# Attention and a mixture of experts on one core: the issue order of all engines worked out by the kernel's own list scheduler

## The chip, the cores and the metric

The kernel runs on one core of a Trainium2 chip. A core has TensorE (PE in the profile; its weight loads are PEld), VectorE (DVE), ScalarE (ACT), GpSimd (POOL) and SyncE (SP), which issues all of this kernel's DMA transfers. Each engine takes its instructions in one fixed order. The metric is the device time of one execution in microseconds; less is better.

## The reference

Two parts are chained. Attention with a local window and block summaries (batch 4, 8 heads, 768 positions, head size 64) gives x, 3072 tokens of 512; a dense mixture of four experts works on x.

```python
k_sum = k.reshape(B, H, nb, block, D).max(axis=3)      # block = 32
v_sum = v.reshape(B, H, nb, block, D).mean(axis=3)
scores_l = scale * q @ k.T      # kept where abs(i - j) < 16, else -1e9
scores_s = scale * q @ k_sum.T + np.log(block)
a = softmax(concat[scores_l, scores_s])
x = a @ concat[v, v_sum]
...
p = domain_probs / (domain_probs.sum(-1, keepdims=True) + 1e-09)
for e in range(4):
    h = np.maximum(x @ w1[e], 0.0)        # 512 -> 1024
    out += p[:, e:e + 1] * (h @ w2[e])    # 1024 -> 512
```

All is float32. The kernel splits operands into a high and a low part and adds three products.

## The kernel before

**Attention** is cut into 64 pieces `n`: batch `n // 16`, 96 queries, four heads. A piece goes through these steps (names as in the code and the profile): `load_piece` (transfers `kr` with keys, `qv` with queries and values), `stage_a` (ACT and POOL split them into `ks`, `qs`, `v12`), `scores` (PE products `psc`, the maximum `nb` on DVE, the exponential `ms` on ACT), `probs` (DVE and ACT write the weights `aw`, high and low), `transposed` (a transposing transfer to `awT`, issued by SP), `values` (PE products `px`), `to_x` (ACT and DVE bring `px` out as `xs`; `xh` and `xl` are its parts). Pieces 0 to 7 have a path of their own (`first_tokens`), with an order written as a table of times (`KEYS`, `STEPS`). Before the pieces of a batch `b` come its summaries: `setup_k` and `setup_v` load eight chunks (`kch`, `vch`), reduce them on DVE (`ksr`, `vsr`, `vmax`), and `setup_v` works out a scale with two small PE steps, `pmx`, and transposes `pvs`.

**The experts** work on blocks of 384 tokens. Blocks 0 and 1 take plain products (`plain_units`): `ph` = w1 x, out as `hh`, `hl`; `po` = w2 h, added into `acc`. Raw weights come in as `wr`, and `w` holds the parts. Blocks 2 to 7 go in three pairs (`pair_units`), whose first product is made with seven half-size products instead of eight (`first`, table `SEVEN`): PSUM banks `pha` to `phd`, with an ACT copy from `pha` to `phb` (the start of the second bank), DVE sums `phb + p` into `phc` and `phd`, and operands `w1g` and `x_t` that ACT, POOL and DVE prepare from `wx` and `xr`. There are 48 such blocks (pair, expert, quarter). The last pair does so for the second product too (`second_sevens`, `poa` to `pod`). Weight scales need two small PE steps per expert, `pmw`.

**What sets the order.** The code interleaves both parts: `advance` issues attention steps up to a position that grows with the expert work done, piece by piece, by the tables `ENDS` and `SHIFT`. The tile framework then orders the instructions of each engine with a scheduler of its own, which may reorder whatever is not pinned by `tc.keep_in_program_order`. Pinned are: everything in the first stage (up to the flags set at lines 1284 and 1289), the loads in `load_chunk` (line 201) and `load_raw` (line 818), and the instructions that prepare w2 in `fetch7` (line 970). Evictions of PSUM in the pairs stand under `tc.high_priority(offset=RUSH)`. All instructions run through the wrapper `Engine` (line 67), so nearly all rows of the profile have its line, L75, and go by tile names. The part that decides on pinning:

```python
def issue(*a, **kw):
    ins = getattr(self.engine, name)(*a, **kw)
    if pinned[self.which]:
        tc.keep_in_program_order(ins)
    return ins
```

`to_x` (line 429) takes the two halves of `px` so: ACT scales half 1 into `xs`, DVE scales half 0 and adds.

Of the kernel before, what the change touches and what calls it, by code (L numbers as in the profile page):

```python
# [2 lines left out]

# [5 lines left out]
F32 = mybir.dt.float32  # L9
F32R = mybir.dt.float32r  # L10
BF16 = mybir.dt.bfloat16
F16 = mybir.dt.float16
AF = mybir.ActivationFunctionType
ALU = mybir.AluOpType
AX = mybir.AxisListType

P = 128
B, H, S, D = 4, 8, 768, 64
# [40 lines left out]
    return min(max(QB * i - WIN, 0), S - KW)  # L59


@with_exitstack
def attn_moe(ctx: ExitStack, tc: tile.TileContext, qvL, qv0, v0L, kD, kT, vT, w1L, w2L, dpL, cst, out):
    nc = tc.nc
    pinned = {"load": True, "rest": True}

    class Engine:


        def __init__(self, engine, which):  # L70
            self.engine, self.which = engine, which

        def __getattr__(self, name):
            def issue(*a, **kw):
                ins = getattr(self.engine, name)(*a, **kw)  # L75
# [6 lines left out]
    V, A, PL, PE = (Engine(e, "rest") for e in (nc.vector, nc.scalar, nc.gpsimd, nc.tensor))  # L82
    SP = Engine(nc.sync, "load")

    def pool(name, bufs=1, **kw):
        return ctx.enter_context(tc.tile_pool(name=name, bufs=bufs, **kw))

    const = pool("const")

    def spare_x(n):  # L90
# [3 lines left out]
    sb = pool("sb")  # L94
# [75 lines left out]
    def mixing():  # L170
        SP.dma_start(pw, dpL)
        s = const.tile([P, NT, 1], F32, name="dps")
# [25 lines left out]
    written = {}  # L198
    st = {}

    def load_chunk(b, hp, ch, src):
        tc.keep_in_program_order(
            nc.sync.dma_start(ch, src[b, 2 * hp : 2 * hp + 2].rearrange("h d s -> (h d) s"))
        )
# [81 lines left out]
    def load_piece(n):  # L286
# [142 lines left out]
    def to_x(n):  # L429
        i, g = (n // 2) % NQ, n % 2  # L430
        tb, ib = n // per, i % (TB // QB)
        pxv = st.pop(n)["px"]
        xs = sb.tile([P, 2, QB], F32, name=f"xs{n}", tag="xt", bufs=2)
        by = 1.0 / ASC if tb < 2 else X_TOP / (ASC * V_TOP)
        A.mul(xs, pxv[:, :, 1, :], by)
        V.scalar_tensor_tensor(xs, pxv[:, :, 0, :], by, xs, op0=ALU.mult, op1=ALU.add)
        if tb < 2:
            if tb not in xT:
                xT[tb] = x_block(tb)
            xh, xl = (x[:, :, ib * QB : (ib + 1) * QB] for x in xT[tb][g])  # L440
# [292 lines left out]
        vmean0.append(v0)  # L733


    RUSH = 200
    SLOW = 0.6
    US1, US2 = 0.175, 0.231

# [78 lines left out]
    def load_raw(e, pr):  # L818
        if (e, pr) in raw_w1 or (e, pr, "1") in stored:
            return  # L820
        raw_w1[e, pr] = []
        for j in range(2):
            raw = sb.tile([P, 512], F32, name=f"wx{e}_{2 * pr + j}", tag="x", bufs=NX)
            tc.keep_in_program_order(nc.sync.dma_start(raw, w1L[e, 2 * pr + j]))
            raw_w1[e, pr].append(raw)

    def w1_operands(e, pr):
# [66 lines left out]
    acc, added = {}, {}  # L894
    scaled_pw = {}
    xpair = {}
    kept = {}
# [44 lines left out]
    es_of = dict(PAIRS)  # L942
    orders, todo, ready = {}, [], {}
# [26 lines left out]
    def fetch7():  # L970
        if todo7:
            e, i = todo7.pop(0)
            pinned["rest"] = True
            w2_operands(e, i, *(("chunk", CHUNKS) if i == 3 and e != es_of[SEVENS[0]][0] else ("x", NX)))
            pinned["rest"] = False

    ready2 = {}

# [116 lines left out]
    def second_sevens(pr, tbs, e, hs):  # L1095
        for t in range(TB // P):
            bank = {}

            def new(k):
                room, tag = dict(a=(ps_sc, "sc"), d=(ps_av, "av")).get(k, (ps_mm, "mm"))  # L1100
                bank[k] = room.tile([P, 512], F32, name=f"po{k}{pr}_{e}_{t}", tag=tag)[:, :256]
                return bank[k]

            gts = [tb * (TB // P) + t for tb in tbs]
            if e == es_of[pr][0]:
                for gt in gts:
                    acc[gt] = sb.tile([P, DM], F32, name=f"acc{gt}", tag="acc", bufs=6)

            def add(row, col, k):
                gt = gts[row]  # L1110
                pe = scaled_pw[e][:, gt % (S // P)]
                to = acc[gt][:, col * 256 : (col + 1) * 256]
                if e == es_of[pr][0]:
                    V.tensor_scalar_mul(to, bank[k], pe)
                else:
                    V.scalar_tensor_tensor(to, bank[k], pe, to, op0=ALU.mult, op1=ALU.add)

            for m, (k, h, w) in enumerate(SEVEN):
# [9 lines left out]
                with tc.high_priority(offset=RUSH):  # L1128
                    if m == 0:
                        A.copy(new("b"), o)  # L1130
                    elif m == 1:
                        five = sb.tile([P, 256], F32, name=f"q5{pr}_{e}_{t}", tag="hs", bufs=2)
                        A.copy(five, o)
                    elif m == 2:
                        V.tensor_tensor(new("c"), o, five, op=ALU.add)
                    elif m == 3:
                        add(0, 0, "a")
                    elif m == 4:
                        V.tensor_tensor(bank["d"], o, five, op=ALU.add)
                        add(1, 1, "d")  # L1140
                    elif m == 5:
                        add(0, 1, "c")
                    else:
                        add(1, 0, "b")
                    if e == es_of[pr][-1] and m > 4:
                        gt = gts[m - 5]
                        SP.dma_start(out[gt * P : (gt + 1) * P, :], acc.pop(gt))
# [43 lines left out]
    def first(pr, tbs, e, hT, w2, room):  # L1191
# [6 lines left out]
            op0=ALU.mult, op1=ALU.mult,  # L1198
        )
        order = orders[pr, e]  # L1200
        for n, i in enumerate(order):
# [6 lines left out]
            bank = {}  # L1208
            at = dict(ops=hT)
# [6 lines left out]
            for m, (k, w, x) in enumerate(SEVEN):  # L1216
                first = m < 2
                o = new(k) if first else bank[k]
# [7 lines left out]
                ahead_of = ExitStack()  # L1226
                ahead_of.enter_context(tc.high_priority(offset=RUSH))
# [20 lines left out]
                ahead_of.close()  # L1248
# [6 lines left out]
    steps = []  # L1255
    for n in range(per, NTB * per):
        k = n + SHIFT * (n >= 2 * per)
# [35 lines left out]
    for (tbs, experts), end in zip(plan, ENDS):  # L1295
        pair = tbs if isinstance(tbs, int) else None
        n = 2 if pair else len(tbs)
# [5 lines left out]
        parts, u, done = None, 0.0, 0.0  # L1303
# [82 lines left out]
```

## Time and profile before

| | |
|---|---|
| median of 3 runs | 1166.38 us (1165.22 to 1167.75) |
| the profiled execution | 1163.23 us, span 1161.5 us |
| PE, DVE, ACT, POOL busy | 1102.4, 818.6, 692.7, 550.8 us |
| mean granted TensorE clock | 0.975 |
| transfers | 184.10 MB, mean 159 GB/s |

An engine's idle time before an instruction stands in brackets with what released it. A row of a stretch gives its bounds, its length, the busy time of PE, PEld, DVE, ACT and POOL with the number of instructions, the granted clock, the DMA share and GB/s.

### The profile page before, as it was taken

Reading aid. Unit: us, or ns where it says so; the run is one execution under the profiler, and the core shown is the slowest. Engines: PE = TensorE matmul, PEld = TensorE weight load, DVE = VectorE, ACT = ScalarE, POOL = GpSimd, SP = SyncE. Lnnn points to the kernel's source line nnn. Section 1 sums busy time; section 2 is a strip of 40 time slices with the busy share of each in tenths; the row PEclk is TensorE's granted clock in tenths of the full one; section 3 lists DMA queues with packets and bytes.
Section 4 is the critical chain, followed back from the end, with each engine's and each line's share of the span. In section 5 each row is a group of like instructions: output and inputs, shape, how many; then the busy total and the mean of one; then the engine's idle time right before and its main releaser. Section 6 shows DMA issues by size and latency. Waiting matters only on the chain.

```text
span 1161.5 us, 20511 instructions
## 1 busy us (share of the span) xinstructions
PE 1102.4 (95%) x6994; PEld 758.6 (65%) x6994; DVE 818.6 (70%) x1959; ACT 692.7 (60%) x1882; POOL 550.8 (47%) x650
## 2 busy tenths in 40 slices
PE   9899688999999789999979999999999999999998
PEld 7788587898896455545544555555555458686867
DVE  6888878875787797676786545456643568787784
ACT  5667466674556888776755445455532356666661
POOL 2587555773744998575653321233300134344340
PEclk9999888999999799999989999999999999999999
DMA  6476756663748599575774536465451142323201
GB/s 241 137 213 179 192 145 184 171 176 89 218 133 212 174 332 311 181 243 166 230 285 120 165 100 191 119 199 152 117 166 36 64 139 80 123 95 125 68 15 55
DMA packets 169305, 184.10 MB, mean 159 GB/s; under 512 B 79344, under 2 KB 115184, under 8 KB 169200
## 3 DMA queue, kind: packets, MB, share of 16 engines
q1 hardware_dynamic: 169200, 182.79, 52.1%
q8 instruction: 55, 0.90, 0.3%
q14 instruction: 50, 0.41, 0.1%
HBM read 131.76 MB, written 34.08 MB: 143 GB/s over the span
## 4 chain that ended last, share of the span: by engine, by line
PE 37%; DVE 6%; DMA 4%; ACT 2%; issue 2%; POOL 1%; SPq 0%; POOLq 0%; ACTq 0%; DVEq 0%
PE po L75 14%; PE phb L75 8%; PE pha L75 5%; PE phc L75 3%; PE phd L75 3%; DVE wr L75 2%; PE poa L75 1%; PE pob L75 1%; PE psc L75 1%; DMA wr<-in_w2L 1%; DVE acc L75 1%; DMA kch<-in_kT 1%; PE pod L75 1%; PE px L75 1%; DMA vch<-in_vT 1%
## 5 line engine op out<-in xcount | busy, mean ns | idle before, releaser
L75 PEld LDWEIGHTS <-w1g 128*128 128x128 f16 x2016 | 196.1, 99 | 155.3 <-issue 21.8
L75 PE MATMUL po<-w2s,h 128*128 128x512 f16 x1152 | 271.2, 379 | 1.2 <-DVE acc L75 0.7
L75 PEld LDWEIGHTS <-h 128*128 128x128 f16 x1584 | 152.4, 98 | 125.9 <-issue 1.4
L75 PE MATMUL phb<-x_t,w1g 128*128 128x384 f16 x864 | 166.2, 330 | 7.3 <-DVE phd L75 4.5
L75 PE MATMUL ph<-xh,w 128*128 128x384 f32 x512 | 144.2, 352 | 10.8 <-ACT xh L75 3.8
L75 POOL TENSOR_TENSOR ks<-kr,ks 128x304 fp32r<-128x304 f32 x112 | 99.3, 892 | 111.3 <-ACT ks L75 110.4
L75 PE MATMUL po<-w,hh 128*128 128x512 f32 x384 | 122.0, 396 | 0.0
L75 ACT ACTIVATE ms<-ms,nb 96x152 f32<-96x152 f32 x256 | 104.3, 415 | 25.6 <-DVE nb L75 24.6
L75 PE MATMUL pha<-x,w1g 128*128 128x384 f16 x576 | 114.5, 333 | 4.9 <-DVE nb L75 4.8
L75 POOL TENSOR_TENSOR w<-wr,w 128x512 fp32r<-128x512 f32 x60 | 81.2, 1363 | 54.9 <-ACT w L75 51.8
L75 PEld LDWEIGHTS ph<-xh,w 128*128 128x128 f32 x512 | 97.9, 197 | 13.4 <-ACT xh L75 4.2
L75 POOL TENSOR_TENSOR v<-qv,v 128x256 f16<-128x256 f32 (+1 forms) x56 | 42.3, 756 | 120.4 <-ACT v L75 108.3
L75 DVE CUSTOM_DVE_ANT_0 ms<-psc,c_sb 96x152 f32<-96x152 f32 x256 | 69.2, 305 | 39.5 <-PE psc L75 36.4
L75 PE MATMUL ph<-xl,w 128*128 128x384 f32 x256 | 89.0, 348 | 0.0
L75 PEld LDWEIGHTS po<-w,hh 128*128 128x128 f32 x384 | 70.9, 189 | 14.6
L75 ACT CAST aw<-ms 96x512 f16<-96x512 f32 x112 | 49.5, 488 | 50.6 <-issue 21.7
L75 DVE TENSOR_TENSOR aw<-ms,aw 96x512 f16<-96x512 f32 x112 | 70.4, 661 | 11.5 <-ACT aw L75 11.2
L75 POOL TENSOR_TENSOR w2g<-wr,w2g 128x256 f16<-128x256 f32 (+1 forms) x32 | 29.5, 939 | 99.6 <-ACT w2g L75 99.3
L75 PE MATMUL po<-w,hl 128*128 128x512 f32 x192 | 76.3, 398 | 0.0
L75 PE MATMUL psc<-ks,qs 128*96 128x152 f32 x448 | 64.9, 271 | 6.6 <-POOL qs L75 3.6
L75 ACT CAST w<-wr 128x512 fp32r<-128x512 f32 x84 | 51.0, 616 | 32.4 <-DMA wr<-in_w1L 21.1
L75 ACT CAST ks<-kr 128x304 fp32r<-128x304 f32 x112 | 48.1, 442 | 33.4 <-PE psc L75 29.7
(184 smaller groups left out, 2251.6 us busy)
## 6 DMA issues: line engine op xcount, KB each, us to landing
wr<-in_w2L SPq DMA_DIRECT2D x104, 256.0 KB, 3.2
qv<-in_qvL SPq DMA_DIRECT2D x56, 320.0 KB, 3.7
kr<-in_kD SPq DMA_DIRECT2D x56, 256.0 KB, 3.2
w1g<-wdg SPq DMA_DIRECT2D x28, 512.0 KB, 3.6
wr<-in_w1L SPq DMA_DIRECT2D x44, 256.0 KB, 3.0
w1g<-wdg SPq DMA_DIRECT2D x28, 384.0 KB, 3.6
wx<-in_w1L SPq DMA_DIRECT2D x32, 256.0 KB, 3.8
wd<-w2s SPq DMA_DIRECT2D x16, 512.0 KB, 5.5
```

The costliest lines, as they stand in the source:

```text
L75: ins = getattr(self.engine, name)(*a, **kw)
```

## The change

The wrapper no longer issues. It appends a `Step` to a list `program`, with the engine, the call, the tiles it writes and reads, and two durations from linear formulas (`takes`, how long the engine is held; `lasts`, until the result is there). At the end `order_of` turns the list into an order, and every instruction is issued in it and pinned:

```diff
 def issue(*a, **kw):
-    ins = getattr(self.engine, name)(*a, **kw)
-    if pinned[self.which]:
-        tc.keep_in_program_order(ins)
-    return ins
+    program.append(Step(self.key, lambda: getattr(self.engine, name)(*a, **kw), name, a, kw))
...
+    for n in order_of(program, bufs_of):
+        tc.keep_in_program_order(program[n].issue())
```

`order_of` has three parts. It finds the dependences from the tiles' footprints and the rotation of each tag's buffers (a new tile waits until all users of the one it replaces are done). It works out due times backwards: PE's steps have their place in program order as a nominal time, and any other step is due by the earliest consumer less durations and waits. Then it lists: each engine takes, at the time it comes free, the ready step with the smallest rank.

```diff
+WAIT = dict(PE=53, ACT=33, DVE=33, POOL=76, SP=28)
+SPARE, SPARE_DMA, LANES = 0.1, 300.0, 8
...
+    def POOL(self, op, kw):
+        n = self.moved()
+        t = 250.0 + 2.1 * n if op == "tensor_tensor" else 100.0 + 1.5 * n
+        return t * (1 + SPARE), t * (1 + SPARE) + 10.0
...
+        due[n] = min(nominal.get(n, math.inf), *d) if d else nominal.get(n, math.inf)
+        if due[n] == math.inf:
+            due[n] = place + 30000.0
+    rank = [nominal.get(n, due[n]) for n in range(len(steps))]
...
+        n = heapq.heappop(waiting[k])[1]
+        s = steps[n]
+        order.append(n)
+        free[k] = t + s.takes
+        if k == "SP":
+            wire = end = max(wire, t + s.lasts[0]) + s.lasts[1]
+            lanes = [*lanes[1:], end]
+        else:
+            end = t + s.lasts
```

The durations of DVE, ACT and POOL are raised by a tenth, transfers by a fifth and 300 ns. All transfers pass one `wire` one after another, eight under way at most. The flags of `pinned` and the blocks under `tc.high_priority` are gone; the tables and `advance` stay, and give the program order that PE's ranks are taken from. In `to_x` the halves change places:

```diff
-        A.mul(xs, pxv[:, :, 1, :], by)
-        V.scalar_tensor_tensor(xs, pxv[:, :, 0, :], by, xs, op0=ALU.mult, op1=ALU.add)
+        A.mul(xs, pxv[:, :, 0, :], by)
+        V.scalar_tensor_tensor(xs, pxv[:, :, 1, :], by, xs, op0=ALU.mult, op1=ALU.add)
```

Both kernels hold the same instructions on every engine; the order differs. In rows of the order, ISA is the operation that adds the mask and takes the maximum of the scores, and the last number in a name only counts tiles.

More of the change, by code (lines that the diff above doesn't have):

```diff
@@ L1 @@
+import heapq
 import math
 from contextlib import ExitStack
+from functools import cache
 import concourse.bass as bass
@@ L59, in _win0, with columns, footprint @@
     return min(max(QB * i - WIN, 0), S - KW)
+BYTES = {F32: 4, F32R: 4, F16: 2, BF16: 2}
+WAIT = dict(PE=53, ACT=33, DVE=33, POOL=76, SP=28)
+SPARE, SPARE_DMA, LANES = 0.1, 300.0, 8
+def columns(ap):
+    return math.prod(n for _, n in ap.ap[1:])
+@cache
+def footprint(offset, pairs, wide):
+    (step, parts), *rest = pairs
+    mask = (1 << wide) - 1
+    for s, n in reversed(rest):
+        if s and n > 1:
+            one, mask = mask, 0
+            for k in range(n):
+                mask |= one << (s * wide * k)
+    return offset // step, offset // step + parts, mask << (offset % step * wide)
@@ new lines, in order_of, with loosen, give @@
+def order_of(steps, bufs):
+    used, live = {}, {}
+    for n, s in enumerate(steps):
+        seen = {}
+        for ap, w in [(x, True) for x in s.written] + [(x, False) for x in s.read]:
+            name, tag = ap.tensor.name, getattr(ap.tensor, "tag", None)
+            if tag is None:
+                continue
+            p0, p1, mask = footprint(ap.offset, ap.ap, BYTES[ap.dtype] // 2)
+            kept = []
+            for at in live.get(name, ()):
+                m, a0, a1, was, wrote = at
+                if m != n and (w or wrote) and a0 < p1 and p0 < a1:
+                    chain = s.key == "PE" == steps[m].key
+                    if was & mask or chain:
+                        full = not chain and (wrote or steps[m].key != s.key)
+                        s.behind[m] = max(s.behind.get(m, False), full)
+                        if w and not was & ~mask and a0 >= p0 and a1 <= p1:
+                            continue
+                kept.append(at)
+            live[name] = [*kept, (n, p0, p1, mask, w)]
+            seen[name] = tag
+        for name, tag in seen.items():
+            used.setdefault(tag, {}).setdefault(name, []).append(n)
+        s.tiles = list(seen.items())
+        for m, full in s.behind.items():
+            steps[m].ahead.append((n, full))
+    queue = {tag: sorted(tiles, key=lambda t: tiles[t][0]) for tag, tiles in used.items()}
+    nominal, now = {}, 0.0
+    for n, s in enumerate(steps):
+        if s.key == "PE":
+            nominal[n] = now
+            now += s.takes
+    freed = {}
+    for tag, names in queue.items():
+        for old, new in zip(names, names[bufs[tag] :]):
+            first = used[tag][new][0]
+            for m in used[tag][old]:
+                if m < first:
+                    freed.setdefault(m, []).append(first)
+    due, place = {}, now
+    for n in range(len(steps) - 1, -1, -1):
+        s = steps[n]
+        place = nominal.get(n, place)
+        end = sum(s.lasts) if s.key == "SP" else s.lasts
+        d = [due[m] - (end + WAIT[steps[m].key] if full else s.takes) for m, full in s.ahead]
+        d += [due[m] - end - WAIT[steps[m].key] for m in freed.get(n, ())]
+        due[n] = min(nominal.get(n, math.inf), *d) if d else nominal.get(n, math.inf)
+        if due[n] == math.inf:
+            due[n] = place + 30000.0
+    rank = [nominal.get(n, due[n]) for n in range(len(steps))]
+    left = [len(s.behind) + len(s.tiles) for s in steps]
+    ready = [0.0] * len(steps)
+    uses = {name: len(at) for tiles in used.values() for name, at in tiles.items()}
+    gone, given = {}, {}
+    coming = {k: [] for k in WAIT}
+    waiting = {k: [] for k in WAIT}
+    free = dict.fromkeys(WAIT, 0.0)
+    lanes, wire, order = [0.0] * LANES, 0.0, []
+    def loosen(n, t):
+        ready[n] = max(ready[n], t)
+        left[n] -= 1
+        if not left[n]:
+            heapq.heappush(coming[steps[n].key], (ready[n], n))
+    def give(tag, t):
+        k = given[tag] = given.get(tag, -1) + 1
+        if k < len(queue[tag]):
+            for n in used[tag][queue[tag][k]]:
+                loosen(n, t + WAIT[steps[n].key] if t else 0.0)
+    for n, s in enumerate(steps):
+        if not left[n]:
+            heapq.heappush(coming[s.key], (0.0, n))
+    for tag in queue:
+        for _ in range(bufs[tag]):
+            give(tag, 0.0)
+    while len(order) < len(steps):
+        best = None
+        for k in WAIT:
+            t = max(free[k], lanes[0] + WAIT[k]) if k == "SP" else free[k]
+            while coming[k] and coming[k][0][0] <= t:
+                n = heapq.heappop(coming[k])[1]
+                heapq.heappush(waiting[k], (rank[n], n))
+            if not waiting[k]:
+                if not coming[k]:
+                    continue
+                t = coming[k][0][0]
+            if best is None or t < best[0]:
+                best = t, k
+        t, k = best
+        while coming[k] and coming[k][0][0] <= t:
+            n = heapq.heappop(coming[k])[1]
+            heapq.heappush(waiting[k], (rank[n], n))
+        n = heapq.heappop(waiting[k])[1]
+        s = steps[n]
+        order.append(n)
[3 more added lines that the diff above has]
+            lanes = [*lanes[1:], end]
+        else:
+            end = t + s.lasts
+        for m, full in s.ahead:
+            loosen(m, end + WAIT[steps[m].key] if full else t + 1.0)
+        for name, tag in s.tiles:
+            uses[name] -= 1
+            gone[name] = max(gone.get(name, 0.0), end)
+            if not uses[name]:
+                give(tag, gone[name])
+    return order
@@ L823, in load_raw @@
             raw = sb.tile([P, 512], F32, name=f"wx{e}_{2 * pr + j}", tag="x", bufs=NX)
[L824 removed]
+            SP.dma_start(raw, w1L[e, 2 * pr + j])
             raw_w1[e, pr].append(raw)
@@ L1127, in second_sevens @@
                     PE.matmul(o, hl, wh, start=False, stop=i == FC // 2 - 1, **again)
[L1128 to L1147, printed above, removed]
+                if m == 0:
+                    A.copy(new("b"), o)
+                elif m == 1:
+                    five = sb.tile([P, 256], F32, name=f"q5{pr}_{e}_{t}", tag="hs", bufs=2)
+                    A.copy(five, o)
+                elif m == 2:
+                    V.tensor_tensor(new("c"), o, five, op=ALU.add)
+                elif m == 3:
+                    add(0, 0, "a")
+                elif m == 4:
+                    V.tensor_tensor(bank["d"], o, five, op=ALU.add)
+                    add(1, 1, "d")
+                elif m == 5:
+                    add(0, 1, "c")
+                else:
+                    add(1, 0, "b")
+                if e == es_of[pr][-1] and m > 4:
+                    gt = gts[m - 5]
+                    SP.dma_start(out[gt * P : (gt + 1) * P, :], acc.pop(gt))
                 if (t, m) in ((0, 3), (0, 6), (1, 2), (1, 5)):
```

92 lines of the change are left out of this document (75 added, 17 removed).

## The prediction

> **What bounds the kernel now.** I read the page first, then busy time by stretches, then the gaps on PE one by one.
>
> ```profile
> PE 1102.4 (95%) x6994; PEld 758.6 (65%) x6994; DVE 818.6 (70%) x1959; ACT 692.7 (60%) x1882; POOL 550.8 (47%) x650
> core 0: 1161.5 us, clock 0.975
> ```
>
> PE is the bound: 1102.4 of 1161.5 us, so 59.1 us idle. It also ran at a mean of 0.975 of its clock, and 0.025 x 1161.5 = 29.0 us of work went to the slow clock. Together 88 us, all that an order alone can win, since no instruction is removed. Where they lie, as us, then busy time of PE, PEld, DVE, ACT, POOL, then granted clock:
>
> ```profile
> 0.00:50.00 50.00, 47.04 (x346) 39.50 (x347) 34.37 (x130) 29.98 (x80) 14.15 (x32) 1.00 0.62 208
> 50.00:250.00 200.00, 175.63 (x1078) 154.58 (x1077) 169.44 (x427) 132.99 (x390) 140.09 (x149) 0.93 0.64 178
> 250.00:350.00 100.00, 100.00 (x614) 90.00 (x614) 72.89 (x199) 54.83 (x158) 49.63 (x55) 1.00 0.54 147
> 350.00:450.00 100.00, 86.24 (x489) 55.87 (x488) 79.79 (x183) 82.74 (x235) 81.23 (x98) 0.91 0.83 255
> 450.00:500.00 50.00, 49.26 (x301) 26.97 (x300) 37.29 (x88) 37.41 (x107) 35.03 (x43) 1.00 0.64 198
> 500.00:650.00 150.00, 137.73 (x801) 74.47 (x799) 110.21 (x262) 96.94 (x275) 82.21 (x102) 0.95 0.66 212
> 650.00:1161.50 511.50, 506.46 (x3374) 317.19 (x3372) 314.63 (x677) 257.77 (x643) 148.45 (x175) 1.00 0.36 110
> ```
>
> Three stages lose. S1, 50 to 250: 24.4 idle and 0.07 x 200 = 14 of clock, 38.4. S2, 350 to 450: 13.8 + 9 = 22.8. S3, 500 to 650: 12.3 + 7.5 = 19.8. (Two-digit clocks make the clock terms 30.5 instead of 29.0.) The rest is the start, 3.0, and the end, 5.0. What ended the long gaps, in brackets (idle us, releaser):
>
> ```profile
> 57.67 0.61 PE L75 MATMUL ph<-xh,w 128*128 128x384 f32 x2 [3.70 <-POOL w L75]
> 131.63 0.61 PE L75 MATMUL px<-awT,v 128*64 128x192 f16 x6 [5.62 <-DMA awT<-aw]
> 134.08 1.65 PE L75 MATMUL ph<-xh,w 128*128 128x384 f32 x4 [1.27 <-ACT xh L75]
> 144.82 0.27 PE L75 MATMUL pmx<-c_sb,vm 128*1 128x128 f32 x1 [2.81 <-DVE vm L75]
> 150.85 1.65 PE L75 MATMUL ph<-xh,w 128*128 128x384 f32 x4 [2.52 <-ACT xh L75]
> 192.32 0.45 PE L75 MATMUL px<-awT,v 128*64 128x192 f16 x3 [3.81 <-DMA awT<-aw]
> 393.60 1.56 PE L75 MATMUL psc<-ks,qs 128*96 128x152 f32 x8 [3.64 <-POOL qs L75]
> 522.27 2.02 PE L75 MATMUL phb<-x_t,w1g 128*128 128x384 f16 x6 [2.75 <-DVE phd L75]
> 595.75 0.56 PE L75 MATMUL psc<-ks,qs 128*96 128x152 f32 x4 [2.20 <-DVE nb L75]
> 599.06 2.08 PE L75 MATMUL pha<-x,w1g 128*128 128x384 f16 x6 [2.75 <-DVE nb L75]
> ```
>
> Six of them are 19.7 of S1's 24.4 us. The releasers are different engines, and none of these is busy for the whole stage: PE waits for things that were done late, behind work that could have waited.
>
> **The change part by part.** The instruction set is the same; its order is new on all five engines.
>
> First, SP, near its 25th transfer: raw weights `wr2`, then keys and values (`kr`, `qv`) of attention piece 8. Before:
>
> ```order
> L75 DMA pw_77<-in_dpL 128x96
> L75 DMA wr20_0_144<-in_w2L 128x512
> L75 DMA wr20_1_146<-in_w2L 128x512
> L75 DMA wr20_2_148<-in_w2L 128x512
> L75 DMA wr20_3_150<-in_w2L 128x512
> L75 DMA kr8_155<-in_kD 128x4x128
> L75 DMA qv8_156<-in_qvL 128x640
> ```
>
> The same place after:
>
> ```order
> L296 DMA qv8_113<-in_qvL 128x640
> L296 DMA kr8_112<-in_kD 128x4x128
> L296 DMA ks0_230<-ksr0_91 64x4x24 x4
> L296 DMA qv9_115<-in_qvL 128x640
> L296 DMA wr20_0_107<-in_w2L 128x512
> L296 DMA kr9_114<-in_kD 128x4x128
> L296 DMA pw_76<-in_dpL 128x96
> ```
>
> Piece 8 now stands ahead of the weights. Before, SP was held for 18.8 us by the four `wr` loads, and `kr` came only then:
>
> ```profile
> 17.21 18.83 SPq L75 DMA_DIRECT2D wr<-in_w2L  x4
> 36.09 0.43 SPq L75 DMA_DIRECT2D kr<-in_kD  x1
> ```
>
> So attention can start up to 18.8 us earlier, and its chain (load, split, scores, softmax, transposed copy, `px`) has that much more cover at 131 and 192.
>
> Second, DVE, where batch 1 is set up (`vsr`, `vmax`: sums and maxima of the value chunks `vch`) between the softmax steps of piece 15. Before:
>
> ```order
> L75 TENSOR_REDUCE vsr1_1748<-vch1_0_1750 128x24
> L75 TENSOR_REDUCE vmax1_1749<-vch1_0_1750 128x1
> L75 TENSOR_SCALAR rs15_1627<-rs15_1627 96x4
> L75 SCALAR_TENSOR_TENSOR xs14_1719<-px14_1693,xs14_1719 128x192
> L75 RECIPROCAL rs15_1627<-rs15_1627 96x4
> L75 TENSOR_TENSOR ms15_1625<-ms15_1625,rs15_1627 96x608
> L75 TENSOR_REDUCE vsr1_1748<-vch1_1_1754 128x24
> L75 TENSOR_REDUCE vmax1_1749<-vch1_1_1754 128x1
> L75 TENSOR_TENSOR aw1_866<-ms15_1625,aw1_866 96x512
> ```
>
> After, the first reductions stand beside piece 11, some hundred rows earlier:
>
> ```order
> L296 TENSOR_REDUCE vsr1_463<-vch1_0_465 128x24
> L296 ISA ms11_325,nb11_326<-psc11_1_331,c_sb_72 96x152
> L296 ISA nb11_326 96x1
> L296 ISA ms11_325,nb11_326<-psc11_1_331,c_sb_72 96x152
> L296 ISA nb11_326 96x1
> L296 TENSOR_REDUCE vmax1_464<-vch1_0_465 128x1
> L296 TENSOR_SCALAR rs11_327<-rs11_327 96x4
> L296 TENSOR_REDUCE vsr1_463<-vch1_1_466 128x24
> ```
>
> In the trace of before, DVE's rows there are
>
> ```profile
> 131.15 0.94 DVE L75 TENSOR_REDUCE vsr<-vch 128x24 f32<-128x768 f32 x1
> 132.01 0.93 DVE L75 TENSOR_REDUCE vmax<-vch 128x1 f32<-128x768 f32 x1
> ...
> 136.45 0.95 DVE L75 TENSOR_REDUCE vsr<-vch 128x24 f32<-128x768 f32 x1 [1.90 <-DMA vch<-in_vT]
> 137.32 0.94 DVE L75 TENSOR_REDUCE vmax<-vch 128x1 f32<-128x768 f32 x1
> 138.18 1.33 DVE L75 TENSOR_TENSOR aw<-ms,aw 96x512 f16<-96x512 f32 x1
> ```
>
> The urgent `aw` waits behind four reductions (3.8 us) and a 1.9 us wait for a late load; `px` of piece 15, then `xh`, follow: the gaps at 144.82 and 150.85 are that queue. They should go.
>
> Third, PE between the last scores of piece 15 and `px` of piece 14, the 5.62 us gap. Before:
>
> ```order
> L75 MATMUL px13_1575<-awT13_1475,vs0_674 64x96
> L75 MATMUL psc15_0_1628<-ks15_0_1560,qs15_1566 96x152 x4
> L75 MATMUL psc15_1_1668<-ks15_1_1563,qs15_1566 96x152 x4
> L75 LDWEIGHTS v12_14_1420
> L75 MATMUL px14_1693<-awT14_1614,v12_14_1420 64x192
> ```
>
> After:
>
> ```order
> L296 MATMUL psc15_1_457<-ks15_1_433,qs15_434 96x152 x4
> L296 MATMUL po0_1_0_440<-w21_3_392,hh0_1_3_388 128x512 x2
> L296 MATMUL po0_1_0_440<-w21_3_392,hl0_1_3_389 128x512
> L296 MATMUL po0_1_1_441<-w21_3_392,hh0_1_3_388 128x512 x2
> L296 MATMUL po0_1_1_441<-w21_3_392,hl0_1_3_389 128x512
> L296 MATMUL po0_1_2_442<-w21_3_392,hh0_1_3_388 128x512 x2
> L296 MATMUL po0_1_2_442<-w21_3_392,hl0_1_3_389 128x512
> L296 MATMUL po0_1_0_440<-w21_4_405,hh0_1_4_396 128x512 x2
> L296 MATMUL po0_1_0_440<-w21_4_405,hl0_1_4_397 128x512
> L296 LDWEIGHTS v12_14_401
> L296 MATMUL px14_458<-awT14_444,v12_14_401 64x192
> ```
>
> Independent products of the same stage now cover the wait.
>
> What S1 gains. Its PE work is 200 - 38.4 = 161.6 us, but DVE is busy 169.4 there. Upper bound: all 38.4. Lower: DVE is the limit, at the best share that a 50 us stretch shows,
>
> ```profile
> 50.00:100.00 50.00, 43.82 (x270) 38.81 (x269) 45.10 (x92) 36.37 (x102) 44.47 (x43) 0.97 0.68 197
> ```
>
> 0.902: 169.4 / 0.902 = 187.8, a gain of 12.2. Over 50 to 350 DVE's 242.3 us stand against 261.6 of PE work, so part can slide into the next stretch, where nothing waits. I take 28, nearer the upper end, because four of the six gaps have their cause moved in the orders above.
>
> S2 prepares the first pair's operands (`w1g`, x parts) beside attention. PE work 77.2; ACT's 82.7 at 0.9 gives 91.9: bounds 8.1 and 22.8. I take 13, near the engine-bound end, because ACT, POOL and DVE are all about 80 here and only 50 to 73 in the stretch before, into which the plan can only move what has buffers.
>
> S3 is batch 3's setup; the chain that ended last runs through its loads:
>
> ```profile
> 566.88 4.64 DMA kch<-in_kT
> 575.00 5.89 DMA kch<-in_kT
> 581.27 7.41 DMA vch<-in_vT
> ```
>
> Batch 3's four `kch` loads stood at SP's rows 378 to 387 and stand now at rows 254 to 337. No engine limits S3 (DVE 110.2, PE work 130.2), so 0 to 19.8; the order moved the chain, so I take 13, two thirds.
>
> The rest must not get worse. In the pair stages (48 blocks) the last `pha` matmul, an ACT copy and `phb` now often have only the six `phd` matmuls between, where the second products of the block before stood too:
>
> ```profile
> L75 PE MATMUL phb<-x_t,w1g x864: 322/326/528, 404.1 to 1133.4; 128*128 128x384 f16 x173
> L75 ACT COPY phb<-pha x48: 463/472/494, 403.5 to 1120.9; 128x384 f32<-128x384 f32 x48
> 1111.79 1.95 PE phb L75 x12
> ```
>
> 0.326 + 0.472 = 0.80 us against six at 1.95 / 12, 0.98: it fits with 0.18 over if ACT is free. I charge 3 us (16 blocks without other cover, four hand-offs each, 0.05). The swapped halves in `to_x` are the same two instructions: 0.
>
> Sum: 28 + 13 + 13 - 3 = 51. Span 1161.5 - 51 = 1110.5; the profiled execution took 1163.23, 1.7 more than its span, and the median of the runs 1166.38, 3.2 more again: **1115.4 us**.
>
> A rule on the clock. A gap of 2.75 us at 522.27 was enough here:
>
> ```profile
> 522.00:526.00 4.00, 3.73 (x19) 2.12 (x19) 3.68 (x10) 2.21 (x6) 1.30 (x2) 0.57 0.95 229
> ```
>
> [...]
>
> **The rivals.**
>
> *DVE stays the limit.* S1 gives 12.2, S2 8.1, S3 13, less 3: 30.3, so 1136.1. For: DVE's 45.10 of 50. Its durations also depend on POOL beside it: the same operation took 917 ns in the first 250 us and 705 later,
>
> ```profile
> L75 DVE TENSOR_TENSOR aw<-ms,aw 96x512 f16<-96x512 f32 x17 | 15.6, 917 | 2.8 <-ACT aw L75 2.6
> L75 DVE TENSOR_TENSOR aw<-ms,aw 96x512 f16<-96x512 f32 x17 | 12.0, 705 | 4.7 <-ACT aw L75 4.7
> 600.00:900.00 300.00, 294.87 (x1785) 160.51 (x1784) 164.83 (x446) 141.11 (x425) 74.54 (x106) 0.99 0.47 137
> ```
>
> with POOL at 0.70 and at 0.25 of the time, while the planner has one figure; pressing POOL's work together makes DVE's longer. [...] Against: the slack after 250.
>
> *Nearly all gaps go.* 38.4 + 22.8 + 19.8 - 3 = 78: 1088.4. For: the planner's durations are close to the rows, here 250 + 2.1 x 512 = 1325 ns against 1363:
>
> ```profile
> L75 POOL TENSOR_TENSOR w<-wr,w 128x512 fp32r<-128x512 f32 x60 | 81.2, 1363 | 54.9 <-ACT w L75 51.8
> ```
>
> Against: S2's engines.
>
> *Slower: the tight hand-offs slip.* Orders stay fixed, and where ACT or DVE has one operation ahead of the copy, PE stands with nothing else queued. 48 blocks with four hand-offs are 192; each slip of 0.4 us (most of a 0.472 copy) costs 77: 1166.4 - 51 + 77 = 1192. It decides from 51 / 192 = 0.27 us a hand-off. Against: 0.18 us to spare, and only a third of the blocks lack other products.
>
> *The plan is the old order in other words:* 1166. Against: the three places above.
>
> **How the numbers follow.** Forecast 0.59, DVE limit 0.18, all gaps gone 0.12, slips 0.08, old order 0.03. The forecast's own range is 1100 to 1130. To hold 8 in 10 it takes in DVE's case and the bounds of S2 and S3, 1150, and reaches down to the case without gaps, 1088. About 0.2% (2.3 us) is what a measurement can tell. Faster is 0.59 + 0.18 + 0.12 = 0.89, same 0.03, slower 0.08.
>
> **What would show it.** Right: `px` no longer waits for `awT` over 2 us; no gap at `pmx` and `xh` of block 1; clock about 0.99; PE idle near 25 to 30 us, most of it in S1 and S2; DVE above 0.85 in S1. Wrong: many gaps of 0.2 to 0.5 us before `phb` and `phc` behind 650 us, where now 5.0 us are idle, or new waits for loads that SP holds back.

## The result and the profile after

The changed kernel took 1110.21 us (median of 4, 1108.39 to 1111.30) and the kernel before, on the same chip, 1166.06 (1165.22 to 1167.75): a ratio of 0.9518, 95% interval 0.950 to 0.9535, so 56 us or 4.8% faster. The forecast was 1115.4. The executions of `start_compute`, an experiment below, fall into two groups 20 us apart, and its ratio is that of the shorter group. Times in the tables are medians; readings of a trace are those of its one profiled execution (1109.61 us for after, 1.8 more than its span).

The page of after, the busy times first, then the span in 40 slices, PE's busy share and its granted clock:

```profile
PE 1093.2 (99%) x6994; PEld 760.3 (69%) x6994; DVE 806.9 (73%) x1959; ACT 695.1 (63%) x1882; POOL 563.8 (51%) x650
PE   8989999999999999999999999999999999999998
PEclk8589999999999999999999999999999999999999
```

PE is busy 1093.2 of 1107.8 us: 14.6 idle where before had 59.1. One digit speaks against so good a picture: the 5 in the second slice of the clock. The same stretches as in the prediction (length; busy us of PE, PEld, DVE, ACT, POOL; granted clock; DMA):

```profile
0.00:50.00 50.00, 44.94 (x242) 35.99 (x243) 23.02 (x105) 21.79 (x59) 10.56 (x29) 0.68 0.55 184
50.00:250.00 200.00, 194.66 (x1237) 172.02 (x1237) 178.32 (x446) 146.34 (x424) 155.92 (x158) 0.97 0.70 190
250.00:350.00 100.00, 100.00 (x616) 88.66 (x615) 86.64 (x238) 60.11 (x180) 52.18 (x60) 1.00 0.64 176
350.00:450.00 100.00, 99.67 (x608) 64.05 (x607) 88.15 (x203) 91.87 (x256) 89.22 (x107) 1.00 0.78 242
450.00:500.00 50.00, 50.00 (x308) 27.47 (x307) 39.59 (x91) 43.43 (x116) 42.03 (x50) 1.00 0.80 246
500.00:650.00 150.00, 150.00 (x914) 81.96 (x913) 105.66 (x271) 96.47 (x276) 70.40 (x90) 1.00 0.71 224
650.00:1107.80 457.80, 453.93 (x3079) 290.15 (x3077) 285.50 (x610) 235.09 (x575) 143.47 (x160) 1.00 0.36 107
```

Idle time and lost clock of each stretch, by the prediction's own measure, and what became of its terms (us). The bounds are times: as everything runs earlier after the change, a stretch does not hold quite the same work in both kernels.

| stretch | before | after | gained | predicted |
|---|---|---|---|---|
| start, 0 to 50 | 3.0 | 5.1 + 0.32 x 50 = 21.1 | -18.1 | 0 |
| S1, 50 to 250 | 38.4 | 5.3 + 0.03 x 200 = 11.3 | 27.1 | 28 |
| S2, 350 to 450 | 22.8 | 0.3 | 22.5 | 13 |
| S3, 500 to 650 | 19.8 | 0 | 19.8 | 13 |
| 250 to 350 and 450 to 500 | 0.7 | 0 | 0.7 | 0 |
| behind 650 | 5.0 | 3.9 | 1.1 | -3 |
| sum | 89.7 | 36.6 | 53.1 | 51 |

The span fell by 53.7. So S2 and S3 gave all they had, the hand-offs cost nothing, and the start took back 18 us that were not in the sum. The longest waits of PE that are left show the same: nothing over 2.1 us, and `px`, which had waited up to 5.62 us for `awT`, waits 0.3. Some rows:

```profile
PE psc L296 <- DVE nb L296: 2.1, 5, 0.7
PE pav L296 <- DVE xt L296: 2.1, 1, 2.1
PE pT L296 <- ACT ms L296: 1.6, 1, 1.6
...
PE psc L296 <- DMA qv<-in_qv: 1.1, 1, 1.1
...
PE phb L296 <- ACT phb L296: 0.3, 1, 0.3
PE px L296 <- DMA awT<-aw: 0.3, 1, 0.3
```

(Columns: who waited for whom, us in total, times, longest.)

Now the start in stretches of 4 us. Before, and then after:

```profile
10.00:14.00 4.00, 4.00 (x34) 3.33 (x33) 2.16 (x9) 1.43 (x5) 0.84 (x3) 1.00 1.05 395
14.00:18.00 4.00, 4.00 (x38) 3.57 (x36) 3.73 (x18) 3.48 (x10) 1.65 (x3) 1.00 1.04 390
18.00:22.00 4.00, 4.00 (x37) 3.54 (x36) 3.40 (x15) 3.09 (x10) 2.03 (x5) 1.00 0.84 275
```

```profile
10.00:14.00 4.00, 3.59 (x23) 2.64 (x22) 1.01 (x5) 1.03 (x3) 1.25 (x4) 1.00 1.05 402
14.00:18.00 4.00, 3.17 (x25) 2.60 (x26) 2.33 (x10) 2.65 (x7) 1.17 (x5) 0.95 1.04 385
18.00:22.00 4.00, 4.00 (x27) 3.70 (x27) 2.61 (x12) 0.48 (x1) 0.52 (x2) 0.50 0.88 282
...
46.00:50.00 4.00, 4.00 (x22) 3.42 (x21) 1.84 (x12) 2.12 (x6) 0.49 (x1) 0.50 0.11 40
54.00:58.00 4.00, 4.00 (x29) 3.76 (x28) 2.61 (x7) 2.83 (x7) 2.22 (x2) 0.86 0.32 92
```

From 18 to about 55 us PE is busy without a gap, at half clock: by the clock records 37.55 us, of which half are lost. (Behind a wait of 2.05 us at 64 us the clock is at half once more, from 65.39 to 72.22 us.) Just ahead of the long stretch PE stood still three times in front of the scores of batch 0 (start, us, idle before and releaser in brackets):

```profile
13.15 0.34 PE L296 MATMUL psc<-ksr,qv 64*96 64x24 f32 x2 [0.41 <-DVE nb L296]
15.17 0.26 PE L296 MATMUL psc<-ksr,qv 64*96 64x24 f32 x1 [0.41 <-DVE nb L296]
16.50 0.34 PE L296 MATMUL psc<-ksr,qv 64*96 64x24 f32 x2 [0.41 <-DVE nb L296]
```

The kernel before has no such gap, though the four products of a bank of scores stand in the same order on PE. What differs is a semaphore. PE's rows for two of the three banks after the change (first halves of pieces 2 and 4), with the waits that they carry:

```
L296 MATMUL psc2_0_122<-k01_78,qv0_1_82 96x128
L296 MATMUL psc2_0_122<-ksr0_91,qv0_1_82 96x24 [waits DVE_49]
...
L296 MATMUL psc4_0_132<-k01_78,qv0_2_83 96x128
L296 MATMUL psc4_0_132<-ksr0_91,qv0_2_83 96x24 [waits DVE_49]
```

`DVE_49` is the semaphore that DVE raises. In before's rows neither product waits. One bank (`psc`) holds two heads in different columns. The planner compares footprints by columns, so it may issue DVE's maximum over the first head ahead of the second head's last product; that product then waits for the maximum to end. The plan knows nothing of that wait.

### The profile page after: what moved, and what is told of

It is laid out like the page before. It is cut to its first block, busy times and chain, and to the rows that moved or that the text cites. A ratio compares the mean times of both kernels' runs of the same rounds, so it can differ in the third digit from the quotient of the medians.

```text
span 1107.8 us, 20496 instructions
## 1 busy us (share of the span) xinstructions
PE 1093.2 (99%) x6994; PEld 760.3 (69%) x6994; DVE 806.9 (73%) x1959; ACT 695.1 (63%) x1882; POOL 563.8 (51%) x650
## 4 chain that ended last, share of the span: by engine, by line
PE 89%; DVE 3%; POOL 2%; DMA 2%; ACT 2%; issue 1%; SPq 0%; POOLq 0%; ACTq 0%; DVEq 0%
PE po L296 30%; PE phb L296 12%; PE ph L296 11%; PE pha L296 8%; PE psc L296 5%; PE pob L296 4%; PE phc L296 4%; PE phd L296 4%; PE poa L296 3%; PE px L296 2%; PE pav L296 2%; PE pod L296 1%; PE poc L296 1%; DMA wr<-in_w1L 1%; PE pT L296 1%
## 5 line engine op out<-in xcount | busy, mean ns | idle before, releaser
L296 PE MATMUL po<-w2s,h 128*128 128x512 f16 x1152 | 279.8, 379 | 0.0
L296 PE MATMUL ph<-xh,w 128*128 128x384 f32 x512 | 141.1, 346 | 0.4 <-ACT xh L296 0.4
L296 POOL TENSOR_TENSOR ks<-kr,ks 128x304 fp32r<-128x304 f32 x112 | 103.3, 926 | 45.5 <-ACT ks L296 38.2
L296 PE MATMUL pha<-x,w1g 128*128 128x384 f16 x576 | 111.5, 326 | 0.0
L296 POOL TENSOR_TENSOR w<-wr,w 128x512 fp32r<-128x512 f32 x60 | 84.0, 1408 | 43.9 <-ACT w L296 38.8
L296 POOL TENSOR_TENSOR qs<-qv,qs 64x384 fp32r<-64x384 f32 x56 | 58.7, 1048 | 91.3 <-ACT qs L296 66.3
L296 PEld LDWEIGHTS ph<-xh,w 128*128 128x128 f32 x512 | 94.8, 192 | 1.3 <-ACT xh L296 0.6
L296 PEld LDWEIGHTS <-hs 128*128 128x128 f16 x576 | 56.3, 98 | 6.6
L296 PEld LDWEIGHTS psc<-ks,qs 128*96 128x96 f32 x448 | 52.7, 164 | 11.5 <-DVE nb L296 1.4
```

The source lines that it names most:

```text
L296: program.append(Step(self.key, lambda: getattr(self.engine, name)(*a, **kw), name, a, kw))
```

## The experiments

My theory on the start after this reading: the small gaps start the half clock, and it costs the 18 us. Rivals: one particular gap (1.55 us at 9.05, in front of the first transpose of softmax rows), the order of the loads, or a clock that falls whatever PE does. The first four runs take these apart.

**One step of PE moved.** The planned order, with one transpose put later:

```
+    turns = [n for n in order if program[n].key == "PE" and program[n].written[0].tensor.name.startswith("pT0")]
+    order.remove(turns[0])
+    order.insert(order.index(turns[1]), turns[0])
```

> The order after the change, with one step of PE put elsewhere: the first transpose of piece 0's softmax rows (pT0) stands just ahead of the second instead of ahead of the folding products (pvf), so that PE no longer stands 1.55 us in front of it while those products are ready. Theory A, the gaps between 6 and 18 us start the half clock, which lasts 37.55 us after the change and costs 18.8 us of work: if this gap decides, the clock stays at 1.00 until 50 us and the time falls from 1110 to about 1091 to 1097. Theory B, the half clock comes of the several smaller gaps together or of something else in the first 18 us: this gap alone gives 0 to 1.6 us and the time stays at 1108 to 1111 with a clock of 0.55 in the first 50 us.

Measured 1111.45 us, ratio 0.9535 (0.9519 to 0.9551): no gain. The move did not remove the idle time ahead of 10 us: PE stood 1.29 us in front of `pvf` instead, for a load (`vn`), and the clock dipped there (0.86 from 6 to 10 us, 0.72 from 10 to 14). But it was back at 1.00 when the three waits of 0.41 us came, which are still there, and fell behind them (`one_moved`):

```profile
14.00:18.00 4.00, 3.04 (x26) 2.23 (x24) 2.00 (x11) 2.03 (x6) 0.81 (x4) 1.00 1.04 388
18.00:22.00 4.00, 3.72 (x23) 3.33 (x23) 2.87 (x10) 1.60 (x5) 0.88 (x3) 0.64 0.90 314
```

So the early gap does not start the long stretch.

**The first stage as recorded, on four engines and on five.** Each step of the first stage is put behind the one recorded before it on its engine; `start_all` has `"SP"` in the list as well.

```
...
+        if s.key in ("PE", "ACT", "DVE", "POOL"):
+            if s.key in last:
+                s.behind.setdefault(last[s.key], False)
+            if n < early:
+                last[s.key] = n
...
```

> The order after the change, with the steps of the first stage (all that is recorded up to the selection of the token rows) kept in recorded order on PE, ACT, DVE and POOL; SP and all that is recorded later are still planned. PE's first 37 us are then full of the same products as in the kernel before, the 40 us of attention start included. If the loss at the start is the planner's order on the engines, the clock is 1.00 in the first 50 us and the time falls by up to 20 us, to 1090 to 1100. If it is the loads' order on SP (first-layer weights land later), the gaps and the half clock stay and the time is 1105 to 1115. If the stage loses what the early start of piece 8 to 15 gave, as I took for S1, it rises to 1118 to 1125.

> As the run with the four engines kept, but SP's transfers of the first stage keep the recorded order too, so that keys and values of piece 8 stand again behind the four raw weight loads. If early loads carry the gain of the first 250 us, as my first term has it, S1 loses again what it won: about 28 us above the run that keeps four engines alone, less what the full clock at the start gives, so 1110 to 1125. If the loads' order matters little and the engines' order carries S1, the two agree within 5 us.

`start_compute` took 1095.0, 1096.8, 1115.3 and 1116.9 us, with clocks of 0.996, 0.995, 0.976 and 0.975; ratio 0.9398 (0.9377 to 0.9419). `start_all` took 1100.38, ratio 0.9434 (0.942 to 0.9449), and all four executions lie within 1.8 us. So the start was indeed worth up to 15 us, and the loads in their old order, the four `wr` loads ahead of piece 8, cost at most 5: my first term rested on them. The two groups are a hint: `start_compute` still had two gaps in front of `psc` (0.41 us of idle time each at 12.44 and 14.53, not the 0.57 that an expectation below has, in its trace, which is one of a short execution; none of a long one is kept), `start_all` none.

**More work in PE's gaps.** 40 products of zeros, ranked last; nothing reads their result.

```
+        for _ in range(FILL):
+            PE.matmul(pz, z[:, 0:P], z, start=True, stop=True)
+            program[-1].filler = True
...
-    rank = [nominal.get(n, due[n]) for n in range(len(steps))]
+    rank = [nominal.get(n, due[n]) + 60000.0 * steps[n].filler for n in range(len(steps))]
...
```

> The order after the change with 40 more products of zeros (128 by 512 each, about 0.217 us, 8.7 us in all, into a result that nothing reads), which the planner puts wherever PE has nothing else ready, most of them in the first 25 us. The outputs are the same; the work is more. If idle gaps start the half clock, the clock holds 1.00 through the first 50 us and the time falls by about 19 us less the products that displace real work (0 to 5 us): 1091 to 1100. If the half clock does not hang on activity, it stays, and the time is that of the change or up to 8.7 us more: 1110 to 1119.

1107.41 us, ratio 0.9505 (0.9477 to 0.9533). The outcome was neither of the two expected. The products filled every gap up to 14 us, but not the three waits, which the plan does not see, and the clock fell behind those (`fillers`):

```profile
10.00:14.00 4.00, 4.00 (x23) 2.95 (x22) 1.32 (x11) 1.63 (x5) 1.30 (x5) 1.00 1.03 399
14.00:18.00 4.00, 3.17 (x27) 2.54 (x26) 1.91 (x10) 2.01 (x6) 1.55 (x6) 1.00 1.05 387
18.00:22.00 4.00, 3.58 (x23) 3.01 (x21) 2.60 (x9) 1.92 (x5) 0.09 (x1) 0.71 0.76 258
38.00:42.00 4.00, 4.00 (x20) 3.39 (x19) 2.10 (x11) 3.65 (x12) 1.44 (x2) 0.50 0.67 172
```

**The three waits alone.** A maximum over a bank is planned behind the last product into that bank. No instruction is added or left out.

```
+        if s.key == "DVE":
+            for x in s.read:
+                if x.tensor.name in banks:
+                    s.behind[banks[x.tensor.name]] = True
+        elif s.key == "PE" and s.written[0].tensor.name.startswith("psc"):
+            banks[s.written[0].tensor.name] = n
```

> The order after the change, with one rule more in the planner: a maximum on DVE that reads a bank of scores (psc) is issued behind all four products of that bank, as it is recorded. After the change three of these maxima are issued between the products of a bank, and the next product then waits for DVE (0.41 us each at 13.15, 15.17 and 16.50). Theory A, these three gaps among small fp32 products start the half clock at 17.9 us: the clock holds 1.00 to about 50 us and the time falls by 15 to 20 us, to 1090 to 1096. Theory B, the waits for the first loads and softmax rows before 10 us (1.08 and 1.55 us) start it: the gaps of 0.41 us go but the half clock stays, and the time is 1107 to 1111.

1090.51 us (1089.15 to 1091.39), ratio 0.9348 (0.9328 to 0.9368): 19.7 us less than after, for three waits of 1.2 us together, and the fastest of all versions here. Theory A. The rule makes the whole plan anew, so later products move too; but PE's first 60 products, up to about 21 us of after, stand in the same order in both. The trace of `psc_whole`:

```profile
6.00:10.00 4.00, 2.60 (x18) 2.51 (x19) 1.33 (x12) 1.00 (x4) 0.40 (x1) 0.69 0.98 354
10.00:14.00 4.00, 4.00 (x11) 2.96 (x11) 0.00 (x0) 0.63 (x3) 1.25 (x4) 0.50 1.04 400
14.00:18.00 4.00, 4.00 (x35) 3.32 (x34) 2.18 (x15) 2.08 (x6) 0.89 (x4) 0.96 1.04 387
18.00:22.00 4.00, 3.79 (x41) 3.20 (x40) 3.36 (x15) 2.10 (x8) 0.80 (x2) 1.00 0.90 312
```

There is a dip here too, behind a wait of 1.96 us for the first queries, but it is over at 14 us, after the twelve `pvf` products (256 columns each), and it does not come back in the stage of small products (behind a wait of 2.09 us at 50 us it does: 0.74 from 50 to 54 us, 0.84 from 54 to 58). The rest of the program keeps the same lead: `pmw`, the first sums of a batch's weights, and the second-layer products `po`, in after and in `psc_whole` (shortest, median and longest duration in ns, first to last start in us):

```profile
L296 PE MATMUL pmw<-c_sb,wm x4: 272/272/272, 165.1 to 340.8; 128*2 128x128 f32 x4
L296 PE MATMUL po<-w2s,h x1152: 379/379/393, 410.1 to 883.6; 128*128 128x512 f16 x192
```

```profile
L302 PE MATMUL pmw<-c_sb,wm x4: 272/272/272, 147.4 to 322.8; 128*2 128x128 f32 x4
L302 PE MATMUL po<-w2s,h x1152: 379/379/393, 391.9 to 865.4; 128*128 128x512 f16 x192
```

165.1 - 147.4 = 17.7, and 18.2 at the last `po`: nearly the whole difference lies ahead of 165 us. By the measure of the table, `psc_whole` loses 6.3 + 0.07 x 50 = 9.8 us in the start and 1.6 + 0.01 x 200 = 3.6 in S1, where after lost 21.1 and 11.3.

**Both.** The first stage as recorded on four engines, with the rule for the banks.

> The run that kept the first stage's steps in recorded order on four engines (1095 to 1117 us, two of four executions in each group), with the maxima behind the whole bank of scores. It had two of these gaps (0.57 us at 12.44 and 14.53). Theory A: without them the half clock of its long executions goes and all executions lie at 1090 to 1097. Theory B, the long executions come of something else (the 4.78 us gap at 50 us): they stay, and the median is anywhere between 1093 and 1117.

1095.86 us (1094.1 to 1096.78), ratio 0.9396 (0.9377 to 0.9414): no execution of four is a long one, as theory A says, though with two of four before it four are few. Against `psc_whole` it is 5.3 slower, so with the clock held the planned order of the first stage is the better one.

**Large products in the slow stretch.** 20 products of zeros, held back until the first score of piece 1 is issued.

```
+    left = [len(s.behind) + len(s.tiles) + s.filler for s in steps]
...
+        if n == mark:
+            for f in range(len(steps)):
+                if steps[f].filler:
+                    loosen(f, t + 1.0)
```

> The order after the change with 20 more products of zeros (128 by 512, bf16, into a result that nothing reads) at one place, behind the first product of piece 1's scores, about 26 us in, when the clock is at half and PE is busy without a gap. The outputs are the same; the work is more, 8.7 us at half clock. Theory A, the clock stays at half there because the small fp32 products load the array too little, and dense products raise it: the clock is 1.00 from about 30 to 35 us on instead of from 55, and the time is 1110 + 8 - 12 = about 1104 to 1110. Theory B, it stays at half for a fixed time of some 37 us whatever PE does: 1116 to 1119.

1100.42 us, ratio 0.944 (0.9416 to 0.9463): 10 us less than after with 20 products more. The row of PE for them, and the stretches around:

```profile
25.88 6.97 PE L303 MATMUL pz<-z 128*128 128x512 bf16 x20
```

```profile
22.00:26.00 4.00, 4.00 (x23) 3.30 (x23) 1.70 (x6) 1.27 (x4) 0.00 (x0) 0.50 0.39 94
26.00:30.00 4.00, 4.00 (x10) 1.38 (x10) 1.41 (x5) 2.43 (x6) 1.57 (x2) 0.50 0.00 0
30.00:34.00 4.00, 3.59 (x18) 1.70 (x16) 0.38 (x3) 0.87 (x3) 0.94 (x2) 0.88 0.49 131
34.00:38.00 4.00, 4.00 (x35) 3.51 (x35) 2.48 (x12) 3.02 (x8) 3.43 (x4) 1.00 0.44 117
```

The clock is back within about 5 us of the first of them. PE was just as busy in the 4 us ahead, with small products. Theory B falls. (That small products load the array too little is the reason that theory A gives, and no run shows it: which property of the twenty brings the clock back, their columns, rows or type, is not taken apart here.) With the 7 us of the products themselves 17 us were won, not 12: a second stretch at half clock behind 60 us went too (the clock of 50 to 250 us is 1.00 in `burst`, 0.97 in after).

The next runs ask which part of the change brings the gain that is there.

**PE's order as recorded.** As above with `("PE",)`, over the whole program; four engines planned.

> PE issues every product in the order in which it is recorded, from start to end; the other four engines keep the planned order. If the gain comes of earlier delivery by SP, DVE, ACT and POOL, nearly all of it stays: 1090 to 1115. If it comes of PE stepping past products that are not ready (the independent products between psc15 and px14, for one), the gaps at px, ph and psc come back and the time is 1135 to 1165. As I took both to matter in S1, where one order place was on PE and two on SP and DVE: 1110 to 1130.

1150.76 us, ratio 0.9859 (0.983 to 0.9888). Its longest waits:

```profile
PE px L301 <- DMA awT<-aw: 9.4, 4, 3.8
PE pmw L301 <- DVE dgw L301: 5.2, 4, 2.6
PE phb L301 <- DVE phc L301: 3.7, 7, 1.1
```

PE stepping past what is not ready carries most of what the plan is worth over the recorded order. That order is not the one that the kernel before issues, which the framework's scheduler had changed, so how much of the 56 us is PE's own is not measured. The clock of `pe_whole`, 0.967 to 0.973 against 0.978 to 0.980 of after, explains some 10 of the 40 us by which it is longer. I had put one of three order places on PE; by this run it deserved the first.

**Two parts put into the kernel before.** One line each: `load_early` of `w2` recorded behind the loads of pieces 8 and 9, and a batch's setup earlier (`setup_k` by 2.0 positions, `setup_v` by 1.85 for batch 1 and 1.2 for the others).

```
-            at(KEYS[12 + fc] - 1e3, load_early, w2L, fc, "2")
+            at(-0.5, load_early, w2L, fc, "2")
```

```
-        steps += [(k - 2.0, setup_k, b), (k - (0.65 if b == 1 else 1.3), setup_v, b)]
+        steps += [(k - 4.0, setup_k, b), (k - 2.5, setup_v, b)]
```

> The kernel before the change, with one part of it alone: on SP the keys and values of pieces 8 and 9 are issued ahead of the four raw second-layer weights wr20, which held SP for 18.8 us. As I argued for S1, attention starts earlier and px waits less for awT (5.62 us at 131.63, 3.81 at 192.32): 5 to 10 us faster, 1156 to 1161. Rival: without a new order on DVE, POOL and ACT behind them the earlier keys wait there instead, or the second-layer weights come late at po: within 3 us of 1166, or some us slower.

> The kernel before the change, with another part alone: the steps that set up a batch (loads of kch and vch, the block sums and maxima on DVE) are recorded about two pieces earlier, so that batch 1's reductions no longer stand between the softmax steps of piece 15. As I argued, the gaps at pmx and ph at 144.82 and 150.85 (5.33 us) go, and part of S3's (the loads of batch 3 on the chain at 566 to 588): 6 to 12 us faster, 1154 to 1160. Rival: the same reductions then stand in front of another piece's steps and the gaps move: within 4 us of 1166.

`before_loads`: 1167.01 us, ratio 0.9992 (0.9972 to 1.0012), nothing. Keys of piece 8 were issued at 16.66 instead of 36.09 us, and the gap that I had tied to them is there unchanged:

```profile
16.66 0.39 SPq L75 DMA_DIRECT2D kr<-in_kD  x1
133.47 0.61 PE L75 MATMUL px<-awT,v 128*64 128x192 f16 x6 [5.61 <-DMA awT<-aw]
```

`before_setup`: 1161.86 us, ratio 0.9961 (0.9941 to 0.9981), 5 us. The gaps at `pmx` and `ph` went, but for 0.32 us, and others came ahead of the scores:

```profile
135.32 0.60 PE L75 MATMUL psc<-ks,qs 128*96 128x152 f32 x2 [5.18 <-POOL qs L75]
148.34 0.74 PE L75 MATMUL psc<-ks,qs 128*96 128x152 f32 x2 [5.23 <-DVE b L75]
```

Moving one thing by hand moved the gap, in this one try. That is the case for planning all engines together.

**Without due times, and with wrong durations.** Both have the rule for the banks. `due_none` ranks the ready steps of four engines by their place in the recorded program; `half_whole` has one number changed.

```
...
+        rank.append(at if s.key in ("SP", "DVE", "ACT", "POOL") else nominal.get(n, due[n]))
```

```
-SPARE, SPARE_DMA, LANES = 0.1, 300.0, 8
+SPARE, SPARE_DMA, LANES = -0.5, 300.0, 8
```

> The planned order with maxima behind the whole bank of scores (1090.5 us), but SP, DVE, ACT and POOL choose among ready steps the one recorded first instead of the one due first. PE still chooses by recorded order among what the plan holds ready. If the due times carry the change, urgent copies and loads stand behind work that could wait, as in the kernel before, and the time is 1115 to 1150. If it is enough that each engine steps past what is not ready (and PE with it), it stays within 10 us: 1090 to 1100.

> The planned order with maxima behind the whole bank of scores (1090.5 us), planned with the durations of DVE, ACT and POOL at about half of what they are (a margin of -0.5 where the change has 0.1). If durations near the traces are what makes the plan hold, PE's fixed order puts products before their operands are there, the gaps of 0.3 to 3 us come back, and the time is 1110 to 1150. If the order hangs on dependencies and due times alone, it is within 8 us: 1088 to 1098.

`due_none`: 1107.02 us (1103.41 to 1119.41), ratio 0.9506 (0.9448 to 0.9564), between my two cases. Its shortest execution had a clock of 0.995, that of `psc_whole`'s profiled execution (1091.39), and was 12 us longer than it: at the same clock that is what the due times bring. The longest, 1119.41 with a clock of 0.977, is the profiled one, and it shows something that theory A does not cover. It went to half clock at 19 us, for 41 us, without any of the three waits; the last wait ahead of it was this one:

```profile
18.01 0.68 PE L305 MATMUL pav<-vsf,sT 96*96 96x260 f32 x2 [0.31 <-DVE sT L305]
18.00:22.00 4.00, 3.99 (x23) 3.66 (x23) 2.01 (x10) 2.16 (x6) 0.00 (x1) 0.62 0.38 142
```

`half_whole`: 1239.65 us, ratio 1.0617 (1.0594 to 1.0641): slower than the kernel before by 72 us, with the same instructions and the same planner.

```profile
PE 1115.4 (90%) x6994; PEld 765.6 (62%) x6994; DVE 802.4 (65%) x1959; ACT 696.6 (56%) x1882; POOL 548.0 (44%) x650
PE phb L302 <- ACT phb L302: 36.5, 19, 4.1
PE psc L302 <- POOL qs L302: 13.9, 6, 5.2
PE pmw L302 <- DVE dgw L302: 11.2, 4, 5.3
PE phb L302 <- DVE phc L302: 9.4, 7, 2.8
```

119.1 us of PE are idle. The waits are those of my slower rival: `phb` behind ACT's copy of `pha` (0.3 us in after), and `psc`, `pmw` behind operands that the plan believed ready.

## Why the prediction was right, and where it was not

*The result* was 5 us from the forecast, inside its own range, but that is luck: two errors of about 20 us cancelled, the 18.1 us of the start and some 20 us that the other stretches gave beyond their terms.

*The start.* The step that failed is "The rest is the start, 3.0, and the end, 5.0", carried through the sum at nothing. It lost 18.1 us. The price of new waits ahead of 50 us was missing: I looked for tight hand-offs in the pair stages alone. `psc_whole`, without the three waits, wins 11.3 of this back, and 7.7 in S1, where the second stretch at half clock goes; `fillers`, with every other gap closed up to 14 us, shows that the three waits are enough for the fall. The 9.8 us that the start of `psc_whole` still loses come of waits ahead of 10 us and near 50 us and of the half clock at 7.5 to 14.3 us.

*S1*, 28 taken, 27.1 measured. The size was met, in part by luck: 6 of the 11.3 us left are half clock (2.6 up to 55.15 us, 3.4 from 65.39 on), and without it and the other waits `psc_whole` gains 34.8. Of its three reasons two did not hold alone. SP's order alone gave nothing (`before_loads`), DVE's place alone 5 us over the whole program (`before_setup`), and PE's order is worth most (`pe_whole`). Issuing the keys earlier, alone, did not move the gap at 131.63; what the three bring together was not taken apart.

*S2*, 13 taken, 22.5 measured: "the engine-bound end" was the wrong end. ACT was to be the limit at 0.9; in after it runs at 0.919 in 350 to 450, with DVE at 0.88 and POOL at 0.89, and PE has 0.3 us idle. The 0.9, about the share that DVE had shown in S1, was no cap here.

*S3*, 13 taken, 19.8 measured, the upper bound: no engine limited it, as the prediction said, and I had still kept a third back for nothing that a row showed.

*Hand-offs*, 3 charged: `phb` waits 0.3 us for ACT in the whole span. The price of the slower rival was real, as `half_whole` shows, but its condition is a plan with wrong durations.

*What would show it.* `px` waits 0.3 us for `awT`, no gap at `pmx` and one of 0.41 us behind `xh`, DVE at 178.32 / 200 = 0.89 in S1: nearly as listed. PE idle was to be 25 to 30 us and is 14.6; the clock was to be 0.99 and is 0.979.

*The rival "nearly all gaps go"*, 0.12, has the better account of everything behind 50 us: `psc_whole`, planned with one rule more against the three waits, took 1090.5, and that rival said 1088.4. I held S2's engines against it.

*The rule on the clock.* In before the clock is at half from 522.37 to 525.78 us, right behind the gap of 2.75 us that ends at 522.27. In the clock records of before and after every change lies a multiple of 3.41 us behind the one before: in after at 17.60, 55.15, 65.39 and 72.22 us, 11, 3 and 2 times that apart. From these distances I estimate that the clock is set anew every 3.41 us, by what PE did in the stretch that ends there; no run tests it. In after, `fillers`, `one_moved`, `burst` and `pe_whole` the stretch of 3.41 us that ends with the fall holds two of the three waits, 0.82 or 0.83 us of idle time. In the short execution of `start_compute` the two gaps lie in two stretches, and so do two gaps of 0.41 us behind 33 us in `burst`; there the clock stays at 1.00. That would explain why `start_compute` came out in two groups, if its stretches begin at another time in each execution, as they do from trace to trace here (the falls at 58.16 us of before and 17.60 of after are 11.9 times 3.41 apart); its long executions left no trace to show it.

What stays open: what decides in such a stretch. PE was not idle throughout when the clock fell: 0.83 us of 3.41 in after. Being busy did not bring the clock back: PE ran without a gap from 18 to 50 us at 0.50. And it is not idle time alone: 1.55 us in front of the first transpose in after, with the `pvf` products right behind, left the clock at 1.00, and in one execution of `due_none` it fell with 0.31 us among small products as the last wait ahead. A threshold was not measured.

## What to carry to other kernels

A plan over all engines was worth more here than the two of its moves that were tried alone, and it stands on its durations: the same planner gave 1090 us with figures near the trace and 1240 with half of them for DVE, ACT and POOL. Whatever the planner believes independent must be independent for the layer that sets the semaphores as well; look for PE rows that wait where the plan has no edge. Read the clock row beside the busy row, above all where PE does small products: there 1.2 us of waits cost 19.7 (after against `psc_whole`).

## What was not expected of the hardware

Half clock held while PE was never idle: from 18 to about 50 us of after PE was busy 4.00 of 4.00 us in each stretch, with fp32 products of 24 to 260 columns, at a clock of 0.50. Twenty bf16 products of 512 columns ended it within about 5 us (`burst`), the twelve `pvf` products of 256 columns likewise (`psc_whole`, 0.50 to 0.96 by 14 to 18 us), and in after it ended some 5 us after the first `ph` products of 384 columns, which come among the small ones from 49.6 us on (0.50 from 50 to 54 us, full from 55.15). The same small products kept full clock where it was there and no gap came: 1.00 and 4.00 of 4.00 us busy from 10 to 37 us of before, where `ph` begins.
